# Two linear-attention layers and two gated layers on one core: where a w_down pass begins, and LayerNorm in thirds

## The chip, the core and the metric

The kernel runs on one core of a Trainium2 chip. The core has five instruction streams: PE (TensorE, matrix products), DVE (VectorE), ACT (ScalarE), POOL (GpSimd) and SP (SyncE), which here issues every DMA. Each stream runs its instructions in the order in which the program has them and waits on semaphores where an instruction needs another engine's result. The kernel keeps its data in one SBUF arena and sums products in eight PSUM banks of 128 x 512 float32. The metric is the device time of one execution in microseconds (us); the median of several runs is compared.

## The reference

```python
x = A_x
x = x + _A_ref(_layernorm(x), A_wqkv, A_wo)
x = x + _B_ref(_layernorm(x), B_w_gate, B_w_up, B_w_down)
x = x + _A_ref(_layernorm(x), A_wqkv, A_wo)
x = x + _B_ref(_layernorm(x), B_w_gate, B_w_up, B_w_down)

def _B_ref(x, w_gate, w_up, w_down):     # x: 1 x 2048 x 1024, F = 3584
    g = einsum("bsd,df->bsf", x, w_gate)
    u = einsum("bsd,df->bsf", x, w_up)
    return einsum("bsf,fd->bsd", g * u, w_down)
```

`_A_ref` is linear attention with 32 heads; the change does not touch its code. The two gated layers use the same weights.

## The kernel before

**Seven products in place of eight.** Every gated matrix product is cut into 2 x 2 blocks and done with seven block products (numbered 1 to 7) and some sums of blocks. In some stages single products of the seven are cut once more in the same way. Such a product is called half-size here: its matmuls have 256 columns in place of 512, there are seven of them (again 1 to 7), and they need sums of quarter blocks first. So "25" in the tables is operation 5 inside product 2.

**Stages.** A gated layer (`layer_B`) works on the 2048 rows in two halves (`ps_` 0 and 1). Each half has a gate/up stage (`gateup`), which writes h = gate * up into the four row blocks hA to hD, and then a w_down pass (`down`), which turns h into rows of x. The first layer's half 0 has no half-size product; gate/up of its half 1 has 5, 4 and 2 half-size (order "542"), and both halves of the second layer have 2, 5 and 4 (order "254"). The w_down passes, except the very first, have 1, 4, 5 and 3 half-size (`DL2`) and 2, 6 and 7 plain.

**Gate/up.** The stage has 28 units of weight columns, handled as 14 pairs. One pair's instructions are written out by hand as a row of tokens in `ORDERS`, and all five streams follow from that row:

- `P1A` is product 1 for the pair's member A (four matmuls of 512 columns), and so on for P1B, P5A, P6A, P7A.
- `21`, `25`, `26`, `27` are the operations of half-size product 2 (two matmuls of 256 each), likewise `51` to `57` and `41` to `47`. Operation 1 writes a bank that ACT copies into the result bank (a seed, L1178); operation 5's result is copied by ACT into SBUF (L1190); after 6 and after 7 DVE adds that copy and writes another seed (L1181). Operation 7 goes on in the bank that the first DVE seed reads, and `D..` (operations 2 and 3, or 4) goes on in the seeded banks.
- `F1A` to `F4B` turn a finished bank into a row of h: a DVE operation (L691), and in odd pairs a POOL multiplication behind it (L1095). F1 writes hA, F4 hB, F2 hC, F3 hD.
- `T0`, `T1` are ticks: places at which other work (a LayerNorm step, a store) is dropped in.
- `R` issues the next two loads of the five-slot weight ring (L420), each with its block sums.
- `S24` and `S5` get the sums of weight blocks for the half-size products: in the first layer four DVE operations (L688) and a store into scratch, later a load from scratch by SP. S24's buffer is double. S5's is double in the second layer's half 1 only; in the second layer's half 0 a new S5 waits until D5A of the pair before has read the old one.
- A prime (`F4A'`) means the pair before, a plus (`S24+`) the next one. The primed tokens of the last pair, the tail, are issued behind the first matmul group of the following w_down pass.
- `H` comes before the last tokens of the last pair and calls `pre()`.

**w_down.** `DORDS` lists the order of the seven products, "1267453" in three passes and "4125637" in the first. A plain product (`plain`, L1483) does four row tiles; a tile has two groups of seven matmuls, over the first and the second half of the rows of h, and is evicted by DVE (L691) into x. The rows of the last pair lie in the second half. A half-size product (`l2prod`, L1553) does its seven operations for two tiles each, in the order of `DOPS`, "1562734". Operation 1 fills bank X; ACT copies it as a seed into the result bank A (L1559). Operation 2 goes on in A, 5 fills bank Y, 6 and 7 go on in X and are copied by ACT, DVE adds Y and the copy into A and B (L1563, `dadd`), 3 and 4 finish A and B, and DVE evicts them. Product 5 is evicted into two targets.

These products need sums of h: small ones of 7 x 128 elements for a half-size product (eight each, DVE L688), large ones of 14 x 128 for the plain ones. They wait in a list, and `POPS` says how many are taken from it behind each step of the pass. Since the pass begins with half-size product 1, `pre()` makes four of its eight sums (those for k = 0 and 1, table `PRE`) at token `H`, before the last seeds of gate/up.

`x_back` loads four row tiles of x back from scratch over the S24 buffer: in the first pass with the tail, in the others when product 1 is nearly done.

**LayerNorm.** Rows for the next layer A are prepared in the ticks of gate/up half 1 of the first layer; the second layer's last rows are prepared in its own gate/up half 0. A step transposes a finished tile (a DMA), normalises the next (L469), and starts a third: two statistics of 512 columns (L447), their aggregate (L451) and two small POOL operations. Ticks 0 and 1 of every second pair do such a step.

## Time and profile before

| | us |
|---|---|
| median of 3 runs (lowest, highest) | 1454.56 (1453.72, 1455.88) |
| the profiled execution | 1453.48 |
| its span, first to last instruction | 1451.8 |
| PE busy, DVE busy in the span | 1442.6, 1145.7 |

The profiled execution's granted TensorE clock is 1.00. The stages in its trace:

| stage | from (us) | to (us) |
|---|---|---|
| layer A, first | 0 | 241 |
| layer 1 half 0: gate/up, w_down | 241, 409 | 409, 495 |
| layer 1 half 1: gate/up "542", w_down | 495, 660 | 660, 739 |
| layer A, second | 739 | 967 |
| layer 2 half 0: gate/up "254", w_down | 967, 1130 | 1130, 1208 |
| layer 2 half 1: gate/up "254", w_down | 1208, 1371 | 1371, 1450 |

A row of the timeline reads: start and duration in us, engine, line, operation, output <- input, shape, count; in brackets the engine's idle time before it and what ended that. L12 is line 12 of the kernel before. PEld is the weight load ahead of a matmul. A matmul's record is longer than the time until the next one may start, so the starts say when PE works and when it waits. A row of the chain has start, length, and what ran. A row of the stretches has the stretch, its length, busy time and count of PE, PEld, DVE, ACT and POOL, the clock, and the DMA share with GB/s.

### The profile page before, as it was taken

What the parts mean: (1) busy time and instruction counts of PE and PEld (TensorE: products, weight loads), DVE (VectorE), ACT (ScalarE), POOL (GpSimd) and SP (SyncE); (2) the same over time, 40 slices, a digit from 0 to 9 for tenths busy, and PEclk for the clock granted to TensorE, in tenths of its full rate; (3) what the DMA queues carried; (4) which work ended last, traced back from release to release, by engine and by line L of the source; (5) the groups of instructions that cost most, each with busy time, mean ns of one, the idle gap of its engine ahead of it and who ended that gap; (6) DMA issues with size and microseconds to landing.
All of it is one profiled execution on the core that took longest, in us unless ns stands there. A gap on an engine that the chain in (4) does not pass through costs nothing.

```text
span 1451.8 us, 22020 instructions
## 1 busy us (share of the span) xinstructions
PE 1442.6 (99%) x8250; PEld 793.5 (55%) x8250; DVE 1145.7 (79%) x2082; ACT 548.6 (38%) x1122; POOL 446.5 (31%) x435
## 2 busy tenths in 40 slices
PE   8999999999999999999999999999999999999999
PEld 4444444444444556665754444446666576666648
DVE  7986988888877797879789869896666986666787
ACT  3332355343400255551123323565555114555402
POOL 5553721222210043432035437214342201342400
DMA  6443757799999899775784646679777769888667
GB/s 232 101 107 103 155 117 187 246 315 312 311 331 305 296 278 288 251 260 194 248 250 111 180 103 156 160 185 269 257 250 250 248 235 287 280 276 271 208 220 234
DMA packets 344539, 329.14 MB, mean 227 GB/s; under 512 B 105200, under 2 KB 290800, under 8 KB 344432
## 3 DMA queue, kind: packets, MB, share of 16 engines
q1 hardware_dynamic: 344432, 327.73, 73.9%
q8 instruction: 65, 1.06, 0.3%
q14 instruction: 42, 0.34, 0.1%
HBM read 244.19 MB, written 62.65 MB: 211 GB/s over the span
## 4 chain that ended last, share of the span: by engine, by line
PE 96%; DVE 2%; DMA 2%; issue 0%; SPq 0%; POOL 0%; ACT 0%; DVEq 0%
PE ps L1071 30%; PE ps L804 15%; PE ps L1483 13%; PE ps L1174 13%; PE ps L1553 8%; PE ps L977 8%; PE ps L891 8%; DMA arena<-in_A_wqkv_dram 1%; DVE arena L447 1%; DMA arena<-in_A_x_dram 1%; PE ps L931 0%; PE ps L903 0%; DVE arena L691 0%; DMA arena<-in_B_w_up_dram 0%; DVE arena L688 0%
## 5 line engine op out<-in xcount | busy, mean ns | idle before, releaser
L1071 PE MATMUL ps<-arena 128*128 128x512 f16 x2128 | 508.1, 379 | 0.0
L691 DVE SCALAR_TENSOR_TENSOR arena<-ps,arena 128x512 f16<-128x512 f32 (+2 forms) x560 | 367.2, 684 | 90.9 <-PE ps L1483 30.5
L1095 POOL TENSOR_TENSOR arena<-arena 128x512 f16<-128x512 f16 x196 | 227.8, 1185 | 475.5 <-DVE arena L691 475.1
L1071 PEld LDWEIGHTS ps<-arena 128*128 128x128 f16 (+1 forms) x2128 | 206.9, 98 | 189.2 <-ACT arena L1076 4.4
L688 DVE TENSOR_TENSOR arena<-arena 128x512 f16<-128x512 bf16 (+6 forms) x532 | 296.4, 598 | 11.3 <-PE ps L1553 3.0
L1076 ACT ACTIVATE arena<-ps 128x512 f32<-128x512 f32 x308 | 184.3, 598 | 165.8 <-PE ps L1071 164.2
L1174 PE MATMUL ps<-arena 128*128 128x256 f16 x1764 | 242.7, 273 | 2.2 <-DVE ps L1181 1.9
L804 PE MATMUL ps<-arena 128*128 128x512 bf16 x1024 | 223.8, 379 | 2.2 <-ACT arena L549 0.9
L1174 PEld LDWEIGHTS ps<-arena 128*128 128x128 f16 (+1 forms) x1764 | 168.7, 98 | 92.0 <-DVE ps L1181 19.7
L1181 DVE TENSOR_TENSOR ps<-ps,arena 128x256 f32<-128x256 f32 x252 | 107.4, 429 | 111.6 <-ACT arena L1190 73.4
L1483 PE MATMUL ps<-arena 128*128 128x512 f16 (+1 forms) x896 | 194.2, 379 | 0.0
L804 PEld LDWEIGHTS ps<-arena 128*128 128x128 f16 x1024 | 99.5, 98 | 121.0 <-DMA arena<-in_A_wqkv_dram 1.5
L1178 ACT COPY ps<-ps 128x256 f32<-128x256 f32 x252 | 88.1, 363 | 175.7 <-PE ps L1174 122.3
L1483 PEld LDWEIGHTS ps<-arena 128*128 128x128 f16 x896 | 87.7, 98 | 105.1
L599 ACT ACTIVATE arena<-ps 128x512 f32<-128x512 f32 x128 | 76.5, 597 | 148.0 <-PE ps L804 125.4
L1553 PE MATMUL ps<-arena 128*128 128x256 f16 (+1 forms) x1176 | 129.9, 273 | 0.0
L1553 PEld LDWEIGHTS ps<-arena 128*128 128x128 f16 x1176 | 115.0, 98 | 14.6
L891 PE MATMUL ps<-arena 128*128 128x512 bf16 x512 | 115.4, 379 | 0.0
L977 PE MATMUL ps<-arena 128*128 128x512 bf16 x512 | 110.8, 379 | 0.0
L833 POOL TENSOR_TENSOR arena<-arena 128x1024 f16<-128x1024 f32 x32 | 79.8, 2494 | 90.3 <-DVE arena L831 83.6
L816 POOL TENSOR_TENSOR arena<-arena 128x512 f32<-128x512 f32 x60 | 76.4, 1274 | 80.2 <-DVE arena L602 78.0
L447 DVE BATCH_NORM_STATS2 arena<-arena 128x6 f32<-128x512 bf16 x128 | 88.2, 689 | 8.3 <-DMA arena<-in_A_x_dram 6.1
(56 smaller groups left out, 787.8 us busy)
## 6 DMA issues: line engine op xcount, KB each, us to landing
arena<-s_scratch SPq DMA_DIRECT2D x84, 512.0 KB, 5.7
arena<-d_images SPq DMA_DIRECT2D x36, 896.0 KB, 5.0
arena<-in_B_w_gate_dram SPq DMA_DIRECT2D x56, 512.0 KB, 4.9
arena<-in_B_w_up_dram SPq DMA_DIRECT2D x56, 512.0 KB, 5.4
arena<-t_scratch SPq DMA_DIRECT2D x20, 896.0 KB, 6.5
s_scratch<-arena SPq DMA_DIRECT2D x28, 512.0 KB, 5.7
arena<-p_scratch SPq DMA_DIRECT2D x28, 512.0 KB, 6.8
arena<-in_A_wqkv_dram SPq DMA_DIRECT2D x12, 1024.0 KB, 8.7
```

The costliest lines, as they stand in the source:

```text
L688: P.add("dve", lambda e: e.tensor_tensor(out=out, in0=a, in1=b, op=op), rd=rd, wr=wr, prd=prd)
L691: P.add("dve", lambda e: e.scalar_tensor_tensor(out=out, in0=a, scalar=sc, in1=b, op0=ALU.mult, op1=op1), rd=rd, wr=wr, prd=prd)
L804: return [e.matmul(psb(bank), xnT[:, k, i * 128:(i + 1) * 128], w[:, k, h * 512:(h + 1) * 512], start=(k == 0), stop=(k == KT - 1)) for k ...
L891: return [e.matmul(psb(bank), xr[:, t, j * 128:(j + 1) * 128], pk[:, h, t, :], start=(t == 0), stop=(t == NST - 1)) for t in range(NST)]
L977: return [e.matmul(psb(bank), xnT[:, g, i * 128:(i + 1) * 128], wp[:, g, dh * 512:(dh + 1) * 512], start=(dh == 0 and g == 0), stop=(g == ...
L1071: P.add("pe", lambda e: [e.matmul(psb(bank), w[:, k, :], x[:, k, :], start=(start and k == 0), stop=(k == 3), skip_group_check=True) for k ...
L1076: P.add("act", lambda e: e.activation(t, psb(bank), AF.Copy, scale=SG), prd=[bank], wr=r)
L1095: P.add(MUL_ENG, lambda e: e.tensor_tensor(out=hx, in0=ut, in1=hx, op=ALU.mult), rd=ur + hr, wr=hr)
L1174: P.add("pe", lambda e: [e.matmul(psb(bank)[:, 256 * half:256 * half + 256], w[:, k, :], xx[:, k, :], start=(start and k == 0), stop=(k == ...
L1181: P.add("dve", lambda e: e.tensor_tensor(out=psb(bank)[:, 256:512], in0=psb(src)[:, 0:256], in1=c5, op=ALU.add), prd=[src], rd=rc5, pwr=[b ...
L1483: return [e.matmul(psb(bank), hv[:, 7 * hf + k, t * 128:(t + 1) * 128], w[:, k, :], start=(q in fresh and hf == 0 and k == 0), stop=(hf == ...
L1553: P.add("pe", lambda e: [e.matmul(half(b, h), x[:, k, :], w[:, k, :], start=(bool(start) and k == 0), stop=(k == 6), skip_group_check=True ...
```

## The change

- w_down passes that began with half-size product 1 begin with plain product 2, and then do product 1 ("2167453").
- A pass's first plain product, also product 4 in the first pass, goes over its four tiles twice: first all tiles with the first half of the rows of h, then all with the second half.
- `pre()` makes no sums any more, since no pass begins with product 1; `POPS` takes product 1's sums behind product 2's tiles, three at each. `H` becomes `HA` and `HB`, which now do nothing.
- `DOPS` becomes "1256734": operation 2 moves ahead of 5 and 6, and its `dadd` behind 6. The stored block images follow that order.
- `x_back` is now issued with the tail in all passes.
- A LayerNorm step is cut into three parts, one per call of `micro`: transpose and normalise; first statistic; second statistic, aggregate and the POOL operations. Two strings say how many parts each tick takes. In the first layer's half 0 three parts follow one another as before.
- The token rows "542" and "254" are reordered.
- A gate/up product 1 of half size is written into the code, but no table uses it; its lines are left out below.

```diff
-        "542": "F4A' 21 25 P1A D3B' F2A' T1' 26 P1B D4B' F3B' F4B' D3A' F3A' 27 51 D2A P6A F1A R D2B F1B 55 56 S24+ T0 P6B 41 H 57 P7A D5A 45 46 P7B D5B F2B 47 S5+ D4A",
-        "254": "D5B' 45' F2A' F2B' P1A 46' F1B' D3A' S24 F3A' S5 47' D4A' F4A' 21 D3B' P1B D4B' 25 26 F4B' T0 F3B' P6A 51 D2A F1A 27 R P6B 55 56 T1 H P7A 41 D2B 57 D5A P7B",
+        "542": "F4A' T1' 21 P1A D3B' F2A' 25 26 P1B D4B' F3B' F4B' D3A' F3A' 27 D2A 51 P6A F1A D2B 55 F1B 56 R P6B T0 41 S24+ 57 P7A HA D5A 45 46 HB P7B D5B S5+ F2B 47 D4A",
+        "254": "D5B' F1B' S5 F2A' HA' 45' 46' F2B' P1A D3A' 47' S24 D4A' F4A' 21 T0 P1B HB' F3A' D3B' D4B' 25 26 F4B' P6A 51 F3B' D2A F1A 27 R T1 P6B 55 56 P7A D2B 41 57 D5A P7B",
...
-    DORDS = {(True, 0): "4125637", (True, 1): "1267453", (False, 0): "1267453", (False, 1): "1267453"}
-    DOPS = "1562734"
+    DORDS = {(True, 0): "4125637", (True, 1): "2167453", (False, 0): "2167453", (False, 1): "2167453"}
+    DOPS = "1256734"
...
-        (True, 1): "1111111 2222 2222 2222 2222211 2222211 2222211 /",
+        (True, 1): "3333 0001102 2222 2222 2222211 2222211 2222211 /",
...
+            def micro(self, lim):
+                self.part += 1
+                if self.part % 3 == 1:
+                    self.step_t(1)
+                    self.b_one()
+                elif self.n < lim and self.half is None:
+                    if self.pending_ab() < 2:
+                        self.half = ln_cnt[0] % 8
+                        ln_cnt[0] += 1
+                        ln_stat(self.order[self.n], self.half, 0)
+                elif self.n < lim:
+                    self.start(self.n)
...
-                def pre():
-                    if "1" in l2:
-                        for k in PRE:
-                            for i in range(2):
-                                need(("s", "1", int(k) - 1, i))
+                def pre(which):
+                    if DORD[0] == "1" and "1" in l2:
...
+                    split = q == DORD[0]
...
+                    if split:
+                        for t in range(4):
+                            half(t, 0)
                     for t in range(4):
                         bank = banks[t]
                         if q in L1N:
                             need((L1N[q], t))
                         for hf in range(2):
...
+                            if not split or hf:
+                                half(t, hf)
...
+                            if op == "6":
+                                dadd(i, 2, A[i])
...
-                        elif op == "2":
-                            dadd(i, 2, A[i])
...
             def ticks0(u):
-                if u % 4 < 2 and not lnp.done():
-                    lnp.flush_step()
+                for _ in range(int(("3300330033003300330033003300" if first else "0000011111011122111111112110")[u])):
+                    if not lnp.done():
+                        lnp.micro(NST)
...
-                if u % 4 < 2 and not is_last and nxt.t_next < LN_G1:
-                    nxt.step_t(1)
-                    nxt.b2_one()
-                    nxt.b1_one()
-                    if nxt.n < LN_G1 and nxt.pending_ab() < 3:
-                        nxt.start(nxt.n)
+                if not is_last:
+                    for _ in range(int("1111111012010211121101111111"[u])):
+                        if nxt.t_next < LN_G1:
+                            nxt.micro(LN_G1)
```

More of the change, by code (lines that the diff above doesn't have):

```diff
@@ L485, in __init__ @@
                 self.depth = 2
+                self.half = None
+                self.part = 0
             def dst(self, n):
@@ L1474, in plain, with half @@
                     img = make_images(q, wsl) if q in mk else []
+                    split = q == DORD[0]
+                    def half(t, hf):
+                        w, rw = wsl[hf]
+                        bank = banks[t]
+                        P.add("pe", lambda e: [e.matmul(psb(bank), hv[:, 7 * hf + k, t * 128:(t + 1) * 128], w[:, k, :],
+                                                        start=(q in fresh and hf == 0 and k == 0), stop=(hf == 1 and k == 6), skip_group_check=True)
+                                               for k in range(7)], rd=rw + rh(ho, t, 7 * hf, 7 * hf + 7), pwr=[bank])
+                        begin()
+                    if split:
+                        for t in range(4):
+                            half(t, 0)
                     for t in range(4):
```

125 lines of the change are left out of this document (82 added, 43 removed), and 6 rows, old and new, of tables (ORDERS, POPS).

## The prediction

> **What bounds the kernel now.** I read the page first, then the chain of waits, then the timeline by stage.
>
> ```profile
> span 1451.8 us, 22020 instructions
> PE 1442.6 (99%) x8250; PEld 793.5 (55%) x8250; DVE 1145.7 (79%) x2082; ACT 548.6 (38%) x1122; POOL 446.5 (31%) x435
> PE 96%; DVE 2%; DMA 2%; issue 0%; SPq 0%; POOL 0%; ACT 0%; DVEq 0%
> ```
>
> PE is the bound, and the change keeps every product, so only time in which PE waits can move. Busy time hides part of that: a matmul's record is longer than its issue interval. The price of one comes from unbroken runs in the chain (start, us, what):
>
> ```profile
> 411.62 83.09 PE ps L1483 x385
> 705.76 24.47 PE ps L1553 x224
> 911.75 55.25 PE ps L977 x256
> 1380.55 36.26 PE ps L1483 x168
> ```
>
> 83.09/385 = 0.2158 us for 512 columns, 24.47/224 = 0.1092 us for 256. A pair of units with three half-size sets has 32 wide and 42 narrow matmuls, 11.49 us; a stage of 14 pairs takes 160.9 us, and the half-size product 1 behind it 98 x 0.1092 = 10.7: 171.6 us from a stage's first matmul to the following plain product. The timeline has the ends:
>
> ```profile
> 494.55 0.60 PE L1174 MATMUL ps<-arena 128*128 128x256 f16 x4
> 669.34 31.03 PE L1483 MATMUL ps<-arena 128*128 128x512 bf16 x143
> 1139.82 36.42 PE L1483 MATMUL ps<-arena 128*128 128x512 bf16 x168
> 1176.08 32.26 PE L1553 MATMUL ps<-arena 128*128 128x256 f16 x294
> ```
>
> Stage I (layer 1, half 1) runs 494.55 to 669.34: 174.8, 3.2 over. Stage II (layer 2, half 0) begins where the L977 run ends, 967.0, and reaches 1139.82: 172.8, 1.2 over. Stage III (layer 2, half 1) begins at 1176.08 + 294 x 0.1092 = 1208.2; the chain's starts lie 0.16 behind the timeline's (L1483 at 1380.55), so 1380.4: 172.2, 0.6 over. III has no LayerNorm; its 0.6 is what a stage costs anyway. So **at most 5.0 us lie here, 0.34% of the run**; that ceiling is what the reader is to see. All other stages keep their order, but for the first halves of layer 1 (below).
>
> **LayerNorm in parts.** One step in stage I:
>
> ```profile
> 525.25 0.54 DVE L469 TENSOR_SCALAR arena<-arena 128x1024 f16<-128x1024 bf16 x1
> 525.71 1.42 DVE L447 BATCH_NORM_STATS2 arena<-arena 128x6 f32<-128x512 bf16 x2
> 525.98 1.03 PE L1071 MATMUL ps<-arena 128*128 128x512 f16 x4
> 527.16 0.21 DVE L451 BATCH_NORM_AGGREGATE arena<-arena 128x2 f32<-128x12 f32 x1
> 527.29 0.73 DVE L1181 TENSOR_TENSOR ps<-ps,arena 128x256 f32<-128x256 f32 x2
> 527.75 1.59 PE L1174 MATMUL ps<-arena 128*128 128x256 f16 x12 [0.75 <-DVE ps L1181]
> ```
>
> Normalise, two statistics and their aggregate hold DVE from 525.25 to 527.29; the seed (L1181) that PE needs is queued behind. PE's four wide matmuls end at 525.98 + 0.86 = 526.84 and it goes on at 527.75: 0.91 lost. After the change the longest part is one statistic with the aggregate, about 0.7 + 0.2 = 0.9 us, against 2.0. Is there room? DVE's load by stage:
>
> ```profile
> 494.70:659.50 164.80, 163.29 (x1045) 99.67 (x1043) 136.52 (x270) 88.99 (x211) 62.46 (x61) 1.00 0.84 265
> 1209.00:1370.60 161.60, 161.49 (x1042) 101.07 (x1041) 102.32 (x199) 87.78 (x210) 58.69 (x52) 1.00 0.79 263
> ```
>
> Third figure: DVE 136.5 of 164.8 in I, 102.3 of 161.6 in III. I has 28 us free over 14 pairs, 2.0 each; the new ticks bring two parts a pair, 0.54 to 0.9 each, mostly 1.4. They fit. In I the tick now stands ahead of the four block sums S24; those cost
>
> ```profile
> 512.25 2.50 DVE L688 TENSOR_TENSOR arena<-arena 128x512 f16<-128x512 bf16 x4
> 523.79 1.55 DVE L688 TENSOR_TENSOR arena<-arena 128x512 f16<-128x512 bf16 x4
> ```
>
> 1.55 alone and 2.50 in pairs where POOL multiplies beside them. Between 56 and D5B, which waits for 57's seed, PE has P6B, 41, 57, P7A, D5A, 45, 46 and P7B, 3.9 us, and 56's own seed takes 0.7 of it: 3.2. A part, the sums and the seed (0.4 of L1181's pair) are 0.9 + 1.55 + 0.4 = 2.9, which fits, or 0.7 + 2.5 + 0.4 = 3.6, which does not. But the tick pushes the sums behind POOL's two multiplications, so I take the short price. By the Trainium skill, page "SBUF — State Buffer", section "SBUF: two separate sides", a DVE operation with two SBUF inputs and a GpSimd operation lock each other out of one shared port pair; by it alone the late pairs would lose about 0.5 us each, four of them 2 us. The trace agrees that the sums stretch (2.50 against 1.55).
>
> **Block sums behind the row writes.**
>
> ```profile
> 650.76 2.27 POOL L1095 TENSOR_TENSOR arena<-arena 128x512 f16<-128x512 f16 x2 [10.31 <-DVE arena L691]
> 653.07 2.23 DVE L688 TENSOR_TENSOR arena<-arena 128x896 f16<-128x896 f16 x4 [0.88 <-POOL arena L1095]
> 654.28 1.03 PE L1071 MATMUL ps<-arena 128*128 128x512 f16 x4
> 655.21 0.76 DVE L1181 TENSOR_TENSOR ps<-ps,arena 128x256 f32<-128x256 f32 x2
> 655.70 1.16 PE L1174 MATMUL ps<-arena 128*128 128x256 f16 x8 [0.39 <-DVE ps L1181]
> 656.90 7.49 POOL L1095 TENSOR_TENSOR arena<-arena 128x512 f16<-128x512 f16 x6 [3.87 <-DVE arena L691]
> ```
>
> The four sums wait for POOL's rows (653.03), the seeds stand behind them, and PE loses 655.70 - 655.14 = 0.56. With product 2 first no sum stands there: gained. Next late are the rows of hB. The pass then begins at 655.70 + 8 x 0.1092 - 0.56 = 656.0; its second sweep wants them after 28 matmuls (6.0 us) and the tail's 1.9 us, at 663.9. POOL works in order, 1.25 us a row; F4B is its fifth of six, at 656.90 - 0.56 + 6.2 = 662.6. Cover 1.3 us; nothing paid, and each us beyond it would be one on PE. In "254" F1B and F2A move ahead and feed POOL sooner. The four x_scratch loads move from product 1 to the tail; SP waits there for the last reader of S24, and the ring loads queued behind it have product 2's 12.1 us: nothing, and as much as SP waits if that were used up.
>
> So I leave 0.4 to each stage for its first pairs, which no tail fills, and 0.1 more to I: I falls from 3.2 to 0.5, II from 1.2 to 0.4, III from 0.6 to 0.4: **-3.7 us.** In steady state I followed each seed to the matmul that needs it in the new "542" and "254": none has less room than before, 46 to 47 gets a product more.
>
> **What is paid.** First DVE in the passes; prices:
>
> ```profile
> 673.50 2.08 DVE L688 TENSOR_TENSOR arena<-arena 128x1792 f16<-128x1792 f16 x2
> 726.22 2.48 DVE L691 SCALAR_TENSOR_TENSOR arena<-ps,arena 128x512 bf16<-128x512 f32 x4
> ```
>
> An eviction 0.6, a sum of 896 0.56 (the 2.23 above), of 1792 1.0. Behind the second sweep stand 4 evictions, 8 small and 4 large sums, 10.9 us, then product 1's own. From the first eviction (0.2 behind the first tile) PE has 4.5 us of sweep and 10.7 of product 1 until plain product 6 asks for the first bank; DVE needs 10.9 + four dadd (1.5, at the 0.37 of L1181's pair) + two S2 sums (2.0) + the eviction 0.6 = 15.0. Level: between nothing and one large sum (1.0) a pass; I take 0.1, nearest to the balance: 0.3.
>
> Second, order "1256734": op 2 follows op 1, so its seed in bank A has one half-op of PE (0.76) to land instead of several. Where product 5 evicts into two targets, product 3's seed is late already:
>
> ```profile
> 705.60 32.26 PE L1553 MATMUL ps<-arena 128*128 128x256 f16 x294
> 728.79 0.36 ACT L1559 COPY ps<-ps 128x256 f32<-128x256 f32 x1 [0.48 <-DVE arena L691]
> 1199.61 0.36 ACT L1559 COPY ps<-ps 128x256 f32<-128x256 f32 x1 [0.81 <-DVE arena L691]
> ```
>
> Product 3 begins at 705.60 + 196 x 0.1092 = 727.00; op 2's second half falls due 21 matmuls later, 729.29; the seed ends at 729.15. Level: 0 to 0.2. In layer 2, half 0: 1176.08 + 217 x 0.1092 = 1199.78, seed ends 1199.97 and a weight load follows: 0.3, up to 0.7 with sums moved ahead of the evictions. Together 0.5 (0 to 1.1).
>
> Third, SP. "254" now puts load S5 ahead of S24; S5 has one buffer in stage II and waits for D5A:
>
> ```profile
> 1040.15 4.70 SPq L420 DMA_DIRECT2D arena<-p_scratch  x2
> 1045.20 0.60 PE L1174 MATMUL ps<-arena 128*128 128x256 f16 x4
> arena<-p_scratch SPq DMA_DIRECT2D x10, 512.0 KB, 6.9
> arena<-p_scratch SPq DMA_DIRECT2D x10, 256.0 KB, 3.5
> GB/s 257 300 365 314 141 303 350 301 38 258 347 312 76 350 373 180 115 357 367 122 160 357 350 100 239 348 342 50 228 344 370 41 344 362 234 83 382 358 96 165
> ```
>
> The first row is S24's and S5's issue, the last the DMA rate in 40 slices of 1000 to 1120. Now S24 (512 KB) is issued at 1040.15 and S5 waits until about 1044.5. After, S24 is issued at 1044.9. Its first reader, 25, comes 16 wide and 16 narrow matmuls behind D5B (1045.20): 5.2 us, 1050.4; so it has 5.5 us. The 6.9 was measured behind four ring loads of 512 KB; S5, issued when those are through, lands in 3.5, and 512 KB more at 350 GB/s add 1.5: 1049.5. Cover 0.9; I take nothing, with 1.4 us x 12 pairs = 17 as the other end. By the Trainium skill, page "DMA: Bandwidth & Descriptors", section "Queues, rings and completion order", each engine consumes a queue's descriptors in ring order and the completion lands after every earlier write; S24 would then land behind S5, as I reckoned.
>
> Fourth, the first pass (plain product 4) in two sweeps delays its first eviction:
>
> ```profile
> 409.08 1.67 PE L1483 MATMUL ps<-arena 128*128 128x512 f16 x7
> 416.93 0.69 DVE L691 SCALAR_TENSOR_TENSOR arena<-ps,arena 128x512 f32<-128x512 f32 x1 [3.58 <-DMA arena<-x_scratch]
> ```
>
> It can start at 409.08 + 0.86 + 5 x 1.51 = 417.5, and now starts at 416.93 for a DMA's sake: 0.6 later, nothing on PE. The half-size gate/up product 1 is in no set, and HA and HB call nothing: no cost.
>
> **Sum:** -3.7 + 0.3 + 0.5 = -2.9 us. The profiled run took 1453.48 (span 1451.8, 1.7 outside it): 1450.6. It lies 1.1 under the median of the runs, 1454.56, which gives **1451.7**.
>
> **Rivals.**
> - *No losses:* seeds and queue come in time, -3.7 to -4.2: 1450.6. For: both were level. Against: layer 2's late seed.
> - *Stalls moved into the passes:* DVE is behind by a large sum in three passes (3.0) and seeds cost 1.1: 1454.56 - 3.7 + 4.1 = 1455.0; by half of it 1453.2. For: DVE has no reserve over those 15 us. Against: it catches up in plain 6.
> - *The parts do not help:* a part still meets sums of 2.5 in four pairs, 0.4 to 0.5 each, 2.0 given back: 1453.7. For: 3.6 against 3.2 above. Against: POOL's two multiplications come before the sums now.
> - *Slower: S24 lands late in stage II.* If its landing stays at 6.9 us, 12 pairs lose 1.4 each: 1468; at 6.2 it is 1460. It decides from 5.5 us; the run is slower than 1457.5 from 6.0. For: the row of 6.9. Against: 3.5 for the load that now precedes it.
>
> **How the numbers follow.** Forecast 0.58 (1450.8 to 1452.8), no losses 0.13, moved stalls 0.14, parts without help 0.06, late S24 0.09. 0.2%, 2.9 us, is about what a measurement of this kernel tells from no change: the line is 1451.65, in the middle of the forecast, which gives it 0.33 and 0.25. Faster 0.33 + 0.13 = 0.46, within 0.25 + 0.14 + 0.06 = 0.45, slower 0.09. The range, 1449.8 to 1455.0, leaves out the late S24 and edges.
>
> **What would show it.** Stage I's first matmul to product 1 of the pass behind it: 160.9 + 12.1 us and at most 0.6 over; no PE wait behind L447's successor; no sums of 896 between 57's seed and D5B; first gap in a pass at product 3's op 2. S24's landing in stage II and PE idle before 25 decide the slower rival. A gain over 5 us would refute the ceiling, and so my reading of the matmul prices.

## The result and the profile after

The changed kernel took 1452.55 us (median of 22 runs, 1451.64 to 1456.31), the kernel before 1454.93 (22 runs beside them, 1453.61 to 1456.58). The ratio over all these runs is 0.9986 with an interval of 0.998 to 0.9993 (the two medians alone would give 0.9984): faster by 0.14%, 2.0 us, clear of no change but inside the 0.2% that the prediction took as its line. The forecast was a ratio of 0.998 and 1451.7 us.

The page of the changed kernel, its head and the shares of its chain of waits:

```profile
span 1450.4 us, 21833 instructions
PE 1439.4 (99%) x8193; PEld 795.5 (55%) x8250; DVE 1135.3 (78%) x2082; ACT 548.9 (38%) x1122; POOL 443.2 (31%) x435
PE 92%; DVE 6%; DMA 1%; ACT 0%; issue 0%; POOL 0%; SPq 0%; DVEq 0%; ACTq 0%
```

The span is 1.4 shorter than the 1451.8 of before. DVE's share of the chain is 6% in place of 2%, but that says little about the change: two lines of layer A, L864 and L867, have 1.4% each in it and under 0.5% before, and no code of layer A changed. In the trace after, 57 of the 8250 matmul records are missing (8193 are counted), so the chain can leave PE there. The shares aren't compared any further; the stages are. Lines have moved: L1483 is L1543 now, L1553 L1623, L1071 L1111, L1174 L1229, L1178 L1233, L1181 L1236, L688 L712, L691 L715, L447 L446, L1559 L1629, L1563 L1633.

The timeline of PE, at the starts of the three gate/up stages, of half-size product 1 behind each, and of plain 6, plain 7 and product 4 in the layer 2 half 0 pass:

```profile
494.89 0.38 PE L1229 MATMUL ps<-arena 128*128 128x256 f16 x2
668.54 10.86 PE L1623 MATMUL ps<-arena 128*128 128x256 bf16 x98
965.17 1.03 PE L1111 MATMUL ps<-arena 128*128 128x512 f16 x4
1139.00 10.86 PE L1623 MATMUL ps<-arena 128*128 128x256 bf16 x98
1149.69 12.25 PE L1543 MATMUL ps<-arena 128*128 128x512 f16 x56
1162.47 12.26 PE L1543 MATMUL ps<-arena 128*128 128x512 f16 x56 [0.53 <-DVE arena L712]
1174.57 23.95 PE L1623 MATMUL ps<-arena 128*128 128x256 f16 x217
1198.78 8.58 PE L1623 MATMUL ps<-arena 128*128 128x256 bf16 x77 [0.26 <-ACT ps L1629]
1207.19 1.03 PE L1111 MATMUL ps<-arena 128*128 128x512 f16 x4
1380.40 10.86 PE L1623 MATMUL ps<-arena 128*128 128x256 bf16 x98
```

With the prediction's base of 160.9 + 12.1 = 173.0 us from a stage's first matmul to product 1: stage I takes 668.54 - 494.89 = 173.65, 0.65 over (3.2 before); II 173.83, 0.8 over (1.4 before, from the first row of the stage; the prediction read 1.2); III 173.21, 0.2 over (0.6). Together 3.5 us less. Two new waits stand in the layer 2 half 0 pass. Plain 6 should end at 1149.69 + 56 x 0.2158 = 1161.78, and plain 7 begins at 1162.47: 0.69. Product 3's second operation starts at 1198.78 in place of 1198.36: 0.42, and 0.09 stands a matmul earlier; with both, product 4 to stage III is 32.62 in place of 32.10. The rest, some 0.9 us, lies in the first layer A (stage I starts 0.34 later) and the second (product 4 to stage II takes 261.75 after, 261.24 before). The change touches no code of layer A, and the runs below that share the pass ahead of it give 261.3 to 261.6 for the second: most of it is scatter.

The same stretches as before (stretch, length, then busy time and count of PE, PEld, DVE, ACT, POOL, the clock, DMA share, GB/s):

```profile
494.70:659.50 164.80, 164.56 (x1052) 101.43 (x1052) 134.09 (x268) 88.43 (x210) 63.69 (x62) 1.00 0.88 269
1209.00:1370.60 161.60, 161.55 (x1038) 101.12 (x1038) 100.59 (x195) 87.40 (x209) 59.59 (x53) 1.00 0.78 258
```

DVE has about the same work in stage I, 134.1 against 136.5; what has changed is the length of its longest turns. One part of a LayerNorm step in the changed kernel, with the block sums and the seed behind it, and the sums of a later pair with no part ahead of them:

```profile
535.51 0.68 DVE L446 BATCH_NORM_STATS2 arena<-arena 128x6 f32<-128x512 bf16 x1
536.11 1.77 DVE L712 TENSOR_TENSOR arena<-arena 128x512 f16<-128x512 bf16 x4
537.80 0.43 DVE L1236 TENSOR_TENSOR ps<-ps,arena 128x256 f32<-128x256 f32 x1
604.62 2.34 DVE L712 TENSOR_TENSOR arena<-arena 128x512 f16<-128x512 bf16 x4
```

### The profile page after: what moved, and what is told of

It reads as the page before. It is cut to its first block, busy times and chain, and to the rows that moved or that the text cites. A ratio compares the mean times of both kernels' runs of the same rounds, so it can differ in the third digit from the quotient of the medians.

```text
span 1450.4 us, 21833 instructions
## 1 busy us (share of the span) xinstructions
PE 1439.4 (99%) x8193; PEld 795.5 (55%) x8250; DVE 1135.3 (78%) x2082; ACT 548.9 (38%) x1122; POOL 443.2 (31%) x435
## 4 chain that ended last, share of the span: by engine, by line
PE 92%; DVE 6%; DMA 1%; ACT 0%; issue 0%; POOL 0%; SPq 0%; DVEq 0%; ACTq 0%
PE ps L1111 31%; PE ps L844 14%; PE ps L1229 13%; PE ps L1543 12%; PE ps L1623 8%; PE ps L1017 8%; PE ps L931 4%; DVE arena L864 1%; DVE arena L867 1%; DMA arena<-in_A_wqkv_dram 1%; DVE arena L712 1%; DVE arena L869 1%; DVE arena L715 1%; DVE arena L871 0%; POOL arena L873 0%
## 5 line engine op out<-in xcount | busy, mean ns | idle before, releaser
L1111 PE MATMUL ps<-arena 128*128 128x512 f16 x2128 | 503.9, 379 | 0.0
L715 DVE SCALAR_TENSOR_TENSOR arena<-ps,arena 128x512 f16<-128x512 f32 (+2 forms) x560 | 363.5, 683 | 84.6 <-PE ps L1543 38.4
L1135 POOL TENSOR_TENSOR arena<-arena 128x512 f16<-128x512 f16 x196 | 224.8, 1170 | 489.2 <-DVE arena L715 488.9
L1111 PEld LDWEIGHTS ps<-arena 128*128 128x128 f16 (+1 forms) x2128 | 207.0, 98 | 194.9 <-ACT arena L1116 4.4
L712 DVE TENSOR_TENSOR arena<-arena 128x512 f16<-128x512 bf16 (+6 forms) x532 | 288.7, 585 | 12.0 <-PE ps L1623 6.7
L1229 PE MATMUL ps<-arena 128*128 128x256 f16 x1764 | 237.8, 273 | 0.3 <-DVE ps L1236 0.2
L1229 PEld LDWEIGHTS ps<-arena 128*128 128x128 f16 (+1 forms) x1764 | 170.2, 98 | 81.9 <-DVE ps L1236 9.7
L1236 DVE TENSOR_TENSOR ps<-ps,arena 128x256 f32<-128x256 f32 x252 | 108.0, 430 | 130.6 <-ACT arena L1245 68.1
L1543 PE MATMUL ps<-arena 128*128 128x512 f16 (+1 forms) x885 | 194.3, 379 | 1.1 <-DVE arena L712 0.5
L1233 ACT COPY ps<-ps 128x256 f32<-128x256 f32 x252 | 88.3, 363 | 168.0 <-PE ps L1229 116.2
L1543 PEld LDWEIGHTS ps<-arena 128*128 128x128 f16 x896 | 87.6, 98 | 105.2 <-DVE arena L712 1.0
L1623 PE MATMUL ps<-arena 128*128 128x256 f16 (+1 forms) x1176 | 129.6, 273 | 0.3 <-ACT ps L1629 0.3
L1623 PEld LDWEIGHTS ps<-arena 128*128 128x128 f16 x1176 | 114.9, 98 | 15.3 <-ACT ps L1629 0.7
L446 DVE BATCH_NORM_STATS2 arena<-arena 128x6 f32<-128x512 bf16 x128 | 88.0, 688 | 8.1 <-DMA arena<-in_A_x_dram 6.2
```

Of the source, the lines that this page charges most:

```text
L712: P.add("dve", lambda e: e.tensor_tensor(out=out, in0=a, in1=b, op=op), rd=rd, wr=wr, prd=prd)
L715: P.add("dve", lambda e: e.scalar_tensor_tensor(out=out, in0=a, scalar=sc, in1=b, op0=ALU.mult, op1=op1), rd=rd, wr=wr, prd=prd)
L1111: P.add("pe", lambda e: [e.matmul(psb(bank), w[:, k, :], x[:, k, :], start=(start and k == 0), stop=(k == 3), skip_group_check=True) for k ...
L1135: P.add(MUL_ENG, lambda e: e.tensor_tensor(out=hx, in0=ut, in1=hx, op=ALU.mult), rd=ur + hr, wr=hr)
L1229: P.add("pe", lambda e: [e.matmul(psb(bank)[:, 256 * half:256 * half + 256], w[:, k, :], xx[:, k, :], start=(start and k == 0), stop=(k == ...
L1236: P.add("dve", lambda e: e.tensor_tensor(out=psb(bank)[:, 256:512], in0=psb(src)[:, 0:256], in1=c5, op=ALU.add), prd=[src], rd=rc5, pwr=[b ...
```

## The experiments

Twelve kernels were run, all as edits of the changed kernel. A single trace shows where a wait is, but some waits on loads come and go between runs, so the time is judged by the ratio. "Over" is a stage's time above its base (173.0 where plain product 2 follows, 171.6 where product 1 does and the end is the plain product behind it); "at 7" and "at 3" are the two waits of the layer 2 half 0 pass. In e1 the record of plain product 2's first matmul is missing in each pass; its weight load shows the start, 0.22 ahead of the first record.

| run | I over | II over | III over | at 7 | at 3 | ratio to before (interval) |
|---|---|---|---|---|---|---|
| before | 3.2 | 1.4 | 0.6 | 0 | 0 | 1 |
| changed | 0.65 | 0.8 | 0.2 | 0.69 | 0.5 | 0.9986 (0.998-0.9993) |
| e1 old pass | 1.4 | 3.6 | 3.4 | 0 | 0 | 1.0022 (1.0013-1.0031) |
| e2 old gate/up | 3.9 | 1.0 | 0.2 | 0.69 | 0.5 | 1.0000 (0.9992-1.0009) |
| e3 operation 2 late | 0.6 | 1.1 | 0.2 | 0.68 | 0 | 1.0006 (0.9997-1.0015) |
| e4 sums in product 4 | 0.85 | 0.7 | 0.2 | 0 | 0.5 | 0.9992 (0.9982-1.0001) |
| e5 S24 first | 1.0 | 0.7 | 0.2 | 0.68 | 0.5 | 0.9989 (0.998-0.9998) |
| e6 one sweep | 4.7 | 5.9 | 6.7 | 0.69 | 0.5 | 1.0098 (1.0083-1.0113) |
| e7 whole steps | 2.4 | 3.4 | 0.2 | 0.69 | 0.5 | 1.0006 (0.9997-1.0015) |
| e8 sums in plain 7 | 1.0 | 1.4 | 0.2 | 0 | 0.5 | 0.9986 (0.9977-0.9995) |
| f1 old 254 and two edits | 1.2 | 0.7 | 0.3 | 0 | 0 | 1.0033 (1.002-1.0045) |
| f2 old rows and two edits | 1.5 | 0.7 | 0.7 | 0 | 0 | 1.0044 (1.0031-1.0056) |
| g1 three edits | 1.4 | 0.7 | 0.8 | 0 | 0 | 0.9989 (0.998-0.9999) |
| g2 parts alone | 3.0 | 0.85 | 0.3 | 0 | 0 | 0.9989 (0.998-0.9998) |

**LayerNorm in parts alone (g2).** Rows, passes, operation order and one sweep as before; PE's order is that of the kernel before, and on DVE only LayerNorm's instructions stand elsewhere.

```diff
-    DORDS = {(True, 0): "4125637", (True, 1): "2167453", (False, 0): "2167453", (False, 1): "2167453"}
-    DOPS = "1256734"
+    DORDS = {(True, 0): "4125637", (True, 1): "1267453", (False, 0): "1267453", (False, 1): "1267453"}
+    DOPS = "1562734"
...
-                    split = q == DORD[0]
+                    split = False
...
```

> The kernel before with LayerNorm in parts alone: token rows, passes, operation order and PE's order as before. Theory A (the parts carry most of the gain, and the new pass order little): stage I falls from 3.2 over to 1.6, of which 0.56 is the block sums at its end; stage II from 1.2 to 0.9; the passes stay as they were: 1.9 less than before, 1452.7, level with the changed kernel. Rival B (the parts need the new rows): stage I 2.6 or more over, 1454 or more. Rival C (the gain is the new passes): no more than 0.5 less than before.

Measured: 1452.78, ratio 0.9989, as much as the whole change within the intervals. Theory A's time is met. Its stage I is not, 3.0 over, so the stages of this one trace don't show the gain that the runs together have (its span is 1451.4, 0.4 under before). The timeline shows one wait that holds half of the 3.0:

```profile
537.57 1.55 DVE L712 TENSOR_TENSOR arena<-arena 128x512 f16<-128x512 bf16 x4 [1.82 <-DMA arena<-in_B_w_gate_dram]
537.84 1.03 PE L1111 MATMUL ps<-arena 128*128 128x512 f16 x4
539.04 0.69 DVE L446 BATCH_NORM_STATS2 arena<-arena 128x6 f32<-128x512 bf16 x1
539.64 0.74 DVE L1236 TENSOR_TENSOR ps<-ps,arena 128x256 f32<-128x256 f32 x2
540.12 1.05 PE L1229 MATMUL ps<-arena 128*128 128x256 f16 x7 [1.25 <-DVE ps L1236]
```

DVE waits 1.82 for a ring load (raw gate weights, for S24's sums), then does the sums, a statistic and the seed, and PE loses 1.41. The load is hardly later than before: it lands 42.4 us after the stage's first matmul, and in the trace of before DVE begins the same sums at 42.1, without a wait. With parts DVE is ready for them 1.5 us sooner. In 8 of the 11 traces with parts DVE waits here, 0.5 to 1.8, and PE loses up to 1.4 (0 in the changed kernel's, 0.4 in f1, 0.6 in f2 and g1, 0.9 in e6); in one of the three with whole steps it waits, 0.3, and PE loses 0.1, though e2 loses 1.5 to the same kind of load two pairs later. So the ring loads can take back part of what the parts gain. The load's own time counts too: 5.8 us from issue to landing here, 4.8 in the changed kernel's trace, 5.0 before. Which of the two decides isn't settled. Without this wait and the 0.10 behind it g2's stage I would be 1.5 over, of which 0.65 are the block sums at its end. By the ratio, **the parts by themselves carry the gain that can be measured**, and rows and passes together add less than these runs can tell: 0.9986 against 0.9989.

**The changed kernel with the old gate/up (e2).** Rows of before and whole LayerNorm steps; the passes stay new.

```diff
-        "254": "D5B' F1B' S5 F2A' HA' 45' 46' F2B' P1A D3A' 47' S24 D4A' F4A' 21 T0 P1B HB' F3A' D3B' D4B' 25 26 F4B' P6A 51 F3B' D2A F1A 27 R T1 P6B 55 56 P7A D2B 41 57 D5A P7B",
+        "254": "D5B' 45' F2A' F2B' P1A 46' F1B' D3A' S24 F3A' S5 47' D4A' F4A' 21 D3B' P1B D4B' 25 26 F4B' T0 F3B' P6A 51 D2A F1A 27 R P6B 55 56 T1 P7A 41 D2B 57 D5A P7B",
...
-                for _ in range(int(("3300330033003300330033003300" if first else "0000011111011122111111112110")[u])):
-                    if not lnp.done():
-                        lnp.micro(NST)
+                if u % 4 < 2 and not lnp.done():
+                    lnp.flush_step()
...
```

> The changed kernel with the gate/up token rows and the whole LayerNorm steps of before; the w_down passes stay new. Theory A: stage I is 2.5 to 2.8 over (3.2 of before less 0.56 for the block sums), stage II 1.1 over, the waits of 0.69 and 0.42 in the layer 2 half 0 pass stay: 1454.3 to 1455.3, level with before. Rival B (the pass order is the gain): about the changed kernel's 1452.5. Rival C: rows and parts matter in stage I only through the DVE queue of the pass, so that stage I is under 1 over.

Measured: 1454.27, ratio 1.0000. Theory A holds: the new passes with the old gate/up bring nothing that can be measured. Stage I is 3.9 over and not 2.7, of which 1.5 is a wait for a ring load. Stage III is 0.2 over with the old rows too, so the rows do nothing there. Of the 0.6 before, 0.27 is a wait at 1213.57, the place where f2 and g1 wait 0.5 and 0.6 for S24's first load, and 0.11 stands at the end, where the block sums were.

**The changed kernel with whole LayerNorm steps (e7).** The edit of the ticks as in e2; rows and passes stay new.

```diff
-                        if nxt.t_next < LN_G1:
-                            nxt.micro(LN_G1)
+                if u % 4 < 2 and not is_last and nxt.t_next < LN_G1:
+                    nxt.step_t(1)
+                    nxt.b2_one()
+                    nxt.b1_one()
+                    if nxt.n < LN_G1 and nxt.pending_ab() < 3:
+                        nxt.start(nxt.n)
...
```

> The changed kernel with whole LayerNorm steps at the first two ticks of every second pair, as before; token rows and passes stay new. Theory A (the parts are what mends stage I): 2 to 3 of the 3.27 us come back, 2.6 to 3.7 over, 1454.5 to 1455.5. Rival B (the rows alone do, since a tick at the head of the pair has room): stage I at most 1.2 over, 1453 or less. Stages II and III: no change by either, as they did not change with the old rows.

Measured: 1454.95, ratio 1.0006: the gain is gone. Stage I is 2.4 over, 1.7 more than with parts, a little short of theory A; rival B falls. That stage II would not change was wrong: 3.4 over. Its waits are LayerNorm's at 970 to 975 (0.65, 0.31, 0.83) and one of 1.35 on S24 at 1110.18, which is the slower rival's mechanism in one pair (below).

**The changed kernel with the old passes (e1).**

```diff
-    DORDS = {(True, 0): "4125637", (True, 1): "2167453", (False, 0): "2167453", (False, 1): "2167453"}
-    DOPS = "1256734"
+    DORDS = {(True, 0): "4125637", (True, 1): "1267453", (False, 0): "1267453", (False, 1): "1267453"}
+    DOPS = "1562734"
...
```

> The changed kernel with the w_down passes of before (half-size product 1 first with its sums ahead of it, operation order 1562734, one sweep), but with the new gate/up token rows and LayerNorm in parts. Theory A (stage I was mended by rows and parts, and the new pass order pays in the layer 2 half 0 pass what it brings): stage I to the plain product behind it is 1.1 to 1.3 over 171.6 in place of 0.68, because the block sums stand ahead of the seeds again; the 0.69 wait at plain product 7 and the 0.42 seed wait of that pass go down to 0.3 together. Sum: equal to the changed kernel within 0.5 us, 1452.0 to 1453.0. Rival B (the pass that begins with plain 2 is the gain): stage I is 2 or more over, 1454.0 or more. Rival C (the new pass order is a plain loss): 1451.5 or less.

Measured: 1457.60, slower than both. Stage I came out nearly as theory A had it (1.4 for 1.1 to 1.3). What nobody had in it is the end of stages II and III: in the new "254" HA stands in the tail behind F1B', where before H stood ahead of it. The timeline at the end of stage II:

```profile
1124.00 2.26 POOL L1135 TENSOR_TENSOR arena<-arena 128x512 f16<-128x512 f16 x2 [2.47 <-DVE arena L715]
1124.90 1.03 PE L1111 MATMUL ps<-arena 128*128 128x512 f16 x4
1125.19 2.09 DVE L712 TENSOR_TENSOR arena<-arena 128x896 f16<-128x896 f16 x2 [0.66 <-POOL arena L1135]
1127.20 0.42 DVE L1236 TENSOR_TENSOR ps<-ps,arena 128x256 f32<-128x256 f32 x1
1127.68 0.50 PE L1229 MATMUL ps<-arena 128*128 128x256 f16 x3 [1.75 <-DVE ps L1236]
```

Product 1's sums wait for POOL's row of F1B', the seed stands behind them, and PE loses 1.92; inside product 1 it loses another 1.0. So the new row "254" needs the pass that begins with product 2: without it, it costs 3 us a stage.

**Operation order 1562734 (e3).** The changed kernel with operation 2 at its old place.

```diff
-    DOPS = "1256734"
+    DOPS = "1562734"
...
```

> The changed kernel with operation order 1562734 in half-size products, as before; all else stays. Theory A (operation 2 directly behind 1 makes product 3's seed late): the 0.42 wait at product 3's operation 2 in the layer 2 half 0 pass goes to 0.1 or less, and no other wait over 0.1 comes in the passes: 0.3 to 0.4 under the changed kernel, 1452.1. Rival B (the late order costs as much elsewhere, since the adds then stand behind operation 2): a wait of 0.2 or more shows at another operation, and the time stays at 1452.5 or rises.

Measured: 1455.45, ratio 1.0006, 2.9 us above the changed kernel by the two ratios. Both halves of the expectation came true at once: the wait at product 3 is gone (32.09 from product 4 to stage III), and each of the three passes has a new one. The timeline in the layer 2 half 0 pass:

```profile
1140.02 2.46 PE L1623 MATMUL ps<-arena 128*128 128x256 bf16 x21
1140.10 0.68 DVE L715 SCALAR_TENSOR_TENSOR arena<-ps,arena 128x512 f32<-128x512 f32 x1
1140.70 2.15 DVE L712 TENSOR_TENSOR arena<-arena 128x896 f16<-128x896 f16 x3
1142.77 0.68 DVE L715 SCALAR_TENSOR_TENSOR arena<-ps,arena 128x512 f32<-128x512 f32 x1
1143.51 8.58 PE L1623 MATMUL ps<-arena 128*128 128x256 f16 x77 [1.04 <-DVE arena L715]
```

Operation 5 writes the bank that held plain product 2's last tile, and that tile's eviction (1142.77) stands behind three sums of the tile before. PE waits 1.20, three times. With operation 2 in between it has 1.5 us of matmuls to do meanwhile. The prediction counted operation 2's move as a cost only; it is what makes product 1 fit behind product 2.

**One sweep (e6).**

```diff
-                    split = q == DORD[0]
+                    split = False
```

> The changed kernel with the first plain product of a pass in one sweep over its tiles. Theory A (the sweeps cover hB's last rows): POOL writes F4B's row about 1.8 us after PE wants it in layer 1 half 1 (fourth of six rows from 655.29, at 659.8 against 658.0) and 3.5 after in layer 2 (third of four rows from 1128.59, at 1131.9 against 1128.4): waits of 1.8, 3.5 and 3.5 at the second matmul group, and since DVE gets its first tile sooner the 0.69 wait at plain product 7 goes: 8.1 more, 1460.6. Rival B (the rows are there, the sweeps only delay the first eviction): the waits are under 0.5 each and the 0.69 goes: 1452 or less.

Measured: 1468.14, 14 us over before. Theory A's waits are there (2.97, 3.60, 3.60 forecast as 1.8, 3.5, 3.5), each on a row of POOL's, but two of them cost more than their length. The last wait, and stretches of 2 us around it:

```profile
1378.26 0.38 PE L1229 MATMUL ps<-arena 128*128 128x256 f16 x2
1382.07 1.46 PE L1543 MATMUL ps<-arena 128*128 128x512 bf16 x3 [3.44 <-POOL arena L1135]
```

```profile
1378.00:1380.00 2.00, 0.64 (x4) 0.20 (x2) 1.93 (x4) 0.00 (x0) 1.85 (x3) 1.00 0.82 226
1380.00:1382.00 2.00, 0.00 (x0) 0.00 (x0) 0.53 (x1) 0.00 (x0) 2.00 (x3) 0.77 0.95 315
1382.00:1384.00 2.00, 1.93 (x5) 0.73 (x6) 0.00 (x0) 0.00 (x0) 1.12 (x2) 0.50 0.89 319
1384.00:1386.00 2.00, 2.00 (x6) 0.71 (x5) 0.72 (x2) 0.00 (x0) 0.00 (x0) 0.50 1.00 382
1386.00:1388.00 2.00, 2.00 (x7) 0.67 (x6) 1.57 (x3) 0.00 (x0) 0.00 (x0) 0.52 0.58 212
1388.00:1390.00 2.00, 2.00 (x11) 0.94 (x10) 0.31 (x1) 0.00 (x0) 0.00 (x0) 1.00 0.00 0
```

The granted clock (third from the right) falls to 0.50 while PE is idle and stays there until about 1388: PE starts 5 to 7 matmuls in 2 us in place of 11. Stage III is 6.5 longer than the changed kernel's: 3.60 of wait, and 2.9 for fourteen matmuls that start about 0.21 late each. In II it is 5.1, with eight such matmuls, 1.6. In I the clock stays at 1.00, and its 4.0 are the 2.97 and a ring load's 0.9. The 0.69 at plain 7 stays, against the expectation: PE is as late as the sums. The two sweeps are worth some 15 us to a pass order that begins with product 2.

**The wait at plain 7 (e4, e8).** It is the sum for tile 0 in S3, the large sums of h that plain 7 multiplies. DVE in plain 6 of the changed kernel (timeline; x3 are two sums and one of the next stage's block sums):

```profile
1153.86 3.22 DVE L712 TENSOR_TENSOR arena<-arena 128x1792 f16<-128x1792 f16 x3
1156.99 0.68 DVE L715 SCALAR_TENSOR_TENSOR arena<-ps,arena 128x512 f32<-128x512 f32 x1
1157.59 3.22 DVE L712 TENSOR_TENSOR arena<-arena 128x1792 f16<-128x1792 f16 x3
1160.73 0.68 DVE L715 SCALAR_TENSOR_TENSOR arena<-ps,arena 128x512 f32<-128x512 f32 x1
1161.33 3.22 DVE L712 TENSOR_TENSOR arena<-arena 128x1792 f16<-128x1792 f16 x3
```

A tile costs DVE 3.7 us and PE 3.0. The eviction at 1160.73 is tile 2's, and S3's first tile is the first sum behind it, ready at 1162.4. e4 puts the block sums into half-size product 4, e8 into plain 7.

```diff
-        (False, 0): "3333 0001102 2222 2222 2222211 2222211 2222211 / 0 0000 1111 0000 0001111 1111111 1",
+        (False, 0): "3333 0001102 2222 2222 2222211 2222211 2222211 / 0 0000 0000 0000 1111111 1111111 1",
```

> The changed kernel with the four block sums for the next gate/up stage (1.04 us each) taken out of plain product 6 of the layer 2 half 0 pass and done in half-size product 4. Theory A (the 0.69 wait at plain product 7 is a DVE queue of three sums of 1792 a tile): the wait goes, 1451.9; product 4 has 2.2 of 11 us of DVE free and gets 3.8 more, so product 5 or 3 may wait, at most 0.4 more than the 0.42 of now. Rival B (the queue only moves): the seed wait of product 3 grows by 0.7 or more and the time stays at 1452.5. Rival C (the wait at 7 is not the sums'): it stays at 0.69.

```diff
-        (False, 0): "3333 0001102 2222 2222 2222211 2222211 2222211 / 0 0000 1111 0000 0001111 1111111 1",
+        (False, 0): "3333 0001102 2222 2222 2222211 2222211 2222211 / 0 0000 0000 1111 0001111 1111111 1",
```

> The changed kernel with the four block sums of 2048 taken out of plain product 6 of the layer 2 half 0 pass and put into plain product 7, where the trace without them shows DVE idle 0.67 a tile. Theory A (the 0.69 wait at plain product 7 is S3's first tile behind two of these sums, and in product 7 nothing of PE waits for them): the wait goes and no wait comes in product 4; DVE is 1.5 us late at the start of product 4, as it is now: 0.7 less, 1451.8. Rival B (product 4's sums come late as with the sums put there): a wait of 0.5 or more at product 4's operation 5, 6 or 7.

Measured: e4 1453.52, e8 1452.17. In both the wait at 7 goes. In e4 it comes back in product 4, 1.25 us, as rival B had it:

```profile
1173.03 9.33 PE L1623 MATMUL ps<-arena 128*128 128x256 f16 x84
1183.45 1.81 PE L1623 MATMUL ps<-arena 128*128 128x256 f16 x15 [1.09 <-DVE ps L1633]
```

In e8 no other takes its place: 35.57 from product 1 to product 4 becomes 34.87, which is 98 x 0.1092 + 112 x 0.2158. The 0.7 is shown in the trace; the ratio, 0.9986, does not resolve it, and that run's trace has 0.69 on S24 besides.

**S24 behind S5 (e5).**

```diff
-        "254": "D5B' F1B' S5 F2A' HA' 45' 46' F2B' P1A D3A' 47' S24 D4A' F4A' 21 T0 P1B HB' F3A' D3B' D4B' 25 26 F4B' P6A 51 F3B' D2A F1A 27 R T1 P6B 55 56 P7A D2B 41 57 D5A P7B",
+        "254": "D5B' F1B' S24 F2A' HA' 45' 46' F2B' P1A D3A' 47' S5 D4A' F4A' 21 T0 P1B HB' F3A' D3B' D4B' 25 26 F4B' P6A 51 F3B' D2A F1A 27 R T1 P6B 55 56 P7A D2B 41 57 D5A P7B",
```

> The changed kernel with S24 and S5 exchanged in token row 254, so that S24 is issued before S5 waits for its buffer, as before the change. Theory A (behind S5 the S24 load lands in 3.9 us and costs PE one wait of 0.14 at 1048.3): S24's landing in the layer 2 half 0 stage goes back to 6 us or more, that wait goes, and the stage gets at most 0.2 shorter; 1452.4. Rival B (the new place pays, because the ring loads or S5 come later otherwise): the stage gets 0.5 or more longer.

Measured: 1452.50, stage II 0.67 over, landing 7.0 us: theory A. The landings in the changed kernel, from 1000 to 1120, and what the late pair looks like in the run e8:

```profile
arena<-p_scratch SPq DMA_DIRECT2D x10, 512.0 KB, 3.9
arena<-p_scratch SPq DMA_DIRECT2D x10, 256.0 KB, 2.7
```

```profile
1043.24 1.57 SPq L422 DMA_DIRECT2D arena<-p_scratch  x2
1044.85 1.24 SPq L552 DMA_TRANSPOSE arena<-arena  x1
1049.80 0.61 PE L1229 MATMUL ps<-arena 128*128 128x256 f16 x4 [0.53 <-DMA arena<-p_scratch]
```

S24 lands in 3.9 us in place of 6.9, so the slower rival is refuted as a loss in every pair. In single pairs it does come late, here with a LayerNorm transpose issued behind it. In stage II, of seven traces with S24 behind S5 (changed, e1, e3, e4, e6, e7, e8) four have such a wait, 0.14 to 1.35; of the seven with S24 first none has. The wait is what the landing takes beyond 5.46 us: 5.6 gave 0.14, 5.84 gave 0.38, 6.15 gave 0.69 and 6.81 gave 1.35. In three of the four it is the same pair, 77 to 79 us into the stage, and there S24 takes 4.5 to 6.2 us in all seven traces; why is open, since the transposes behind other pairs cost nothing.

**Rows and parts, and product 3 (f1, f2, g1).** In all three the block sums stand in plain 7 and product 3 does 1526734, with the others at 1256734. f1 has the old "254", f2 both old rows, g1 the new rows with S24 first. In f1 and f2 the loads of layer A's weights stand ahead of product 3's operation 2 in layer 1 half 1 and overwrite its ring slot, so that this operation multiplies by layer A's weights; g1 keeps them behind it.

```diff
-                    for n, op in enumerate(DOPS):
+                    for n, op in enumerate("1526734" if q == "3" else DOPS):
...
-                        if n % 2 == 1 or n == 6:
+                        if n in ((2, 3, 5, 6) if q == "3" else (1, 3, 5, 6)):
```

In g1 also:

```diff
-                        if q == "3" and op == "5" and not is_last and ps_:
+                        if q == "3" and n == 2 and not is_last and ps_:
```

> The changed kernel with three edits: token row 254 as before the change (542 stays new), the four block sums of 2048 in plain product 7 of the layer 2 half 0 pass, and product 3 doing its operations as 1526734 while the others keep 1256734. Theory A (row 254 brought nothing and exposes S24, the other two waits are DVE queues): no wait on S24 in the layer 2 half 0 stage, and 0.7 or less over for the stage (0.97 with whole steps); no wait at plain product 7; the 0.42 seed wait at product 3's operation 2 goes to 0.1 or less. Sum: 1.3 to 1.6 under the changed kernel, 1451.0 to 1451.3. Rival B (the new row 254 is what lets the parts fit): the stage is 1.5 or more over and the time is 1452.5 or more. Rival C (product 3's wait is the eviction of its bank and not the place of operation 2): 0.3 or more stays there, at operation 2 or at 5.

> As the run beside it, with token row 542 of before as well, so old rows with LayerNorm in parts. It is the fourth corner for stage I: old rows with whole steps were 5.3 over 171.6 to product 1 at its base of 171.6 (3.95 over the 173.0 of the new pass), new rows with whole steps 2.4 over 173.0, new rows with parts 0.68. Theory A (rows and parts each bring their share, 1.5 and 1.7): 2.0 to 2.6 over 173.0, 1.5 to 2 us above the run beside it. Rival B (the parts alone do it): 1.0 or less over, level with the run beside it. Rival C (parts at the old tick places collide with the sums): 3 or more over.

> The changed kernel with three edits: S24 issued before S5 in token row 254; the four block sums of 2048 in plain product 7 of the layer 2 half 0 pass; product 3 doing its operations as 1526734, with the loads of layer A's weights still behind its third operation, so that operation 2 reads its ring slot before they overwrite it. Theory A (the three waits are separate, each with its own cause): no wait on S24, none at plain product 7, none over 0.1 at product 3; 0.14 + 0.69 + 0.51 less than the changed kernel, 1451.2, and a span of 1449.1 plus the startup's scatter of 0.5. Rival B (one of them comes back elsewhere in the same pass, as with the sums put into product 4): a new wait of 0.4 or more in the layer 2 half 0 pass and 1452 or more.

Measured: f1 1459.31, f2 1460.86, g1 1452.95. All waits at 7 and 3 are gone. f1 and f2 lose 6.8 and 6.9 where operation 2 waits for the weights, and 1.6 and 1.3 more at a clock of 0.50 behind that; so their times say little else, but their stages do. Stage II with the old "254" and parts is 0.7 over, as good as the new row without its S24 risk. Stage I with old rows and parts is 1.5, with the new row 1.2, both with the wait for a ring load (0.7 and 0.5). That is nearest to rival B of f2, the parts do it: without the wait 0.8 and 0.7. f2's time is 1.5 above f1's, as its theory A had it, but the two intervals overlap, and the stages account for 0.7 of it. In g1 the gain was given back in another place than rival B had it:

```profile
730.06 5.22 SPq L422 DMA_DIRECT2D arena<-in_A_wqkv_dram  x4
739.42 1.90 PE L844 MATMUL ps<-arena 128*128 128x512 bf16 x8 [1.54 <-DMA arena<-in_A_wqkv_dram]
```

The load of layer A's weights goes into operation 2's slot, so it is issued one operation later, at 730.06 against 728.06 in the changed kernel (whose trace is 0.5 ahead at that point), and PE waits 1.7 for it against at most 0.65 in the runs with the load at its old place. A kernel with g1's edits, but 1526734 in layer 2 alone, was not run.

## Why the prediction was right, point by point

- **The ceiling** held: 5.0 us of waits forecast in the three stages, 5.2 by the table, of which 3.5 went.
- **LayerNorm in parts** was the right mechanism and the largest term. It is shown both ways, by the ratios: put into the kernel before it brings 0.11% (0.02 to 0.20), taken out of the changed one it costs what the change brought. 0.65 over in stage I against a forecast of 0.5; stage II fell by 0.55 against 0.8: a pair at 994.93 to 995.47 still loses 0.44. The short price for the sums was the right choice: behind a part they took 1.5 to 1.8 us in all five pairs, and 2.1 to 2.5 only in five pairs that have no part ahead of the sums and lose nothing behind them; one part, at 512.37, was itself stretched to 1.22, without a wait on PE. So the rival "the parts do not help" fell by its own condition. What neither saw is that DVE, being earlier, can meet the ring loads (g2).
- **Block sums behind the row writes**: 0.56 and 0.10 at 655.70 are gone, and the rows of hB come in time. What the sweeps hide the forecast did not work out; by e6 it is 3.0 to 3.6 us of wait in each pass, and in two of them 1.6 and 2.9 more by the clock. Stage III fell by 0.4 against a forecast of 0.2 partly by luck: 0.27 of it is a load that was late in the one trace of before. With what the passes lose at other places, the new pass order by itself gains nothing that can be measured (e2).
- **DVE's queue in the passes**, 0.1 a pass, was mis-sized: 0, 0.69 and 0, the second inside its bounds of 0 to 1.0. The working stopped at plain product 6's first bank. The queue was level there, and the next tile rate decided: in layer 2 half 0 plain 6 carries one more sum a tile, 3.7 against 3.0 us.
- **Seeds at operation 2**: 0.5 forecast, 0.5 measured, at the place named and in the pass named. What the step missed is that the same move saves 1.2 a pass (e3). The sum was not spoilt, because the step stood in it as the change has it.
- **S24 behind S5**: nothing forecast; 0.4 a run on the mean of seven traces (0 to 1.35, one pair each). The room was reckoned well, 5.5 us against 5.46. The landing is shorter than reckoned, 3.9 us in place of 4.6 (1044.9 to 1049.5); what the working left out is that single pairs land later than the rest.
- **The first pass and `x_back`**: nothing forecast, nothing measured (83.09 us from the first pass's plain product 4 to stage I, before and after).
- **The sum**: -3.5 in the stages, +1.2 in the passes, +0.9 in layer A, most of it scatter, -1.4 in the two traces; by the ratio -2.0 against -2.9 forecast. The direction and the parts were right; the missing 0.9 is the queue (0.4 more), stage II (0.3 less) and scatter. By the medians, 2.4 us apart, 0.5 is missing.

Not settled: why DVE waits up to 1.8 us for one ring load in stage I in some runs with parts and not in others. Whether new rows and passes bring anything beyond the parts lies below what these runs resolve.

## What to carry to other kernels

Where the engine that bounds a kernel depends on another that is busy four fifths of the time, cut the longest turn in that other engine's queue before reordering the work around it: the cut alone brought as much here, within the noise, as the cut with everything else. Before moving an operation, ask of each neighbour which bank or buffer it writes and who must have emptied it; the same move can cost at one place and save at another. And where a queue only just keeps up, follow it into the next product, whose work for a tile may be more, and not only to the first deadline.

## What the runs showed of the hardware

A pause of PE can cost more than its length. Pauses of 1.92 us (e1) and 2.97 us (e6) left the granted clock at 1.00. Two of 3.60 us (e6) and one of 6.8 (f1) took it to 0.50, and it stayed there for 3.3 us, 5.9 us and 3.7 us after PE had begun again; that cost 1.6, 2.9 and 1.6 us on top. In all, the clock stood at 0.50 for 3.4 us in the first case and for 6.8 in the two others. The Trainium skill, page "TensorE: Matmul & The Clock Gate", section "What's actually happening", says that the PE clock is gated to half after at least one idle window of about 3.4 us and released after about as much sustained work, with a window that runs freely. The traces agree with the length: 2.97 us was too short, 3.60 enough, and the clock was low for one such window or for two. The 5.9 us shows that the way back can take longer than one window.
